# Masked attention and a rational feed-forward layer on one core: a third block in parts, another order of score products, another decoding of weights

## The chip, the core and the metric

The kernel runs on one core of a Trainium2 chip. The metric is the time of one execution on the device, in microseconds. The engines of the core have these names in the profile: PE is TensorE (products), PEld is TensorE's loading of weights, DVE is VectorE, ACT is ScalarE, POOL is GpSimd, SP is SyncE. Each engine works through its own list of instructions in order.

## The reference

Eight batches of eight heads, 576 positions, 64 values per head. A score below its row's maximum minus `tau` is dropped before the softmax. The output of the attention, 4608 rows of 512, goes through two layers with a rational function between them.

```python
scores = scale * np.matmul(q, k.transpose(0, 1, 3, 2))
thresh = np.max(scores, axis=-1, keepdims=True) - tau
scores = np.where(scores >= thresh, scores, -1000000000.0)
attn = np.exp(scores - np.max(scores, axis=-1, keepdims=True))
attn = attn / (np.sum(attn, axis=-1, keepdims=True) + 1e-09)
x = np.matmul(attn, v)                    # then to (4608, 512)
h = x @ w_in                              # (4608, 2048)
P = a[0] + a[1] * h + a[2] * h**2 + a[3] * h**3
Q = 1.0 + np.abs(b[0]) * np.abs(h) + np.abs(b[1]) * h**2
out = (P / (Q + 1e-6)) @ w_out            # (4608, 512)
```

The weights `w_in` and `w_out` come to the kernel as 64-bit floats, seen as pairs of 32-bit words.

## The kernel before

The kernel does not write its instructions down in order. It makes a list of small operations, each with an engine (or several that could take it, with a duration for each, in `FLEX`), a key that says how early it is wanted, the operations that it must follow, and the buffers that it takes and gives back. `Plan.order` then places them one by one on the engines by these assumed durations and latencies (`LAT`, `OWN`, `TO`), and the resulting order is the order of the instructions. Constants at the top (`WHEN`, `SPACING`, `EARLY`, `PRICE`, `TOL` and others) set the keys, the preference between engines, and how far a wanted operation may go before one that could start sooner.

**Attention.** A unit is 128 query positions of a pair of heads (four such units per pair, and half a unit for the remaining 64 positions). There are 128 full units. Its scores are made by `f_qk`: two products with 64 rows each, one for each head, on the two row halves of PE (L776; in float32 each shows as two records), and one product with all 128 rows for the remaining 64 keys of both heads (L780). Then DVE takes the maximum (L786), ACT applies threshold and exponential (L801, L805), the weights of the softmax are split in a high and a low f16 part (`f_hi`, L303 on ACT or L305 on DVE, and `f_lo`, L827), are transposed by DMA, and multiplied with V in column halves of PE (`f_av`, L896). For the first pairs the transposition is done by PE in float32 (`f_tr`, `f_avp`). V is split too (`vh`, `vl`, `vc`); the buffers of V need their empty corners set to zero again before each use (`f_zero`, L683, on DVE).

**Steps.** The two layers are done for 256 rows at a time (a chunk; 18 of them) and four blocks of 128 hidden units (a step, `moe_ops`). 72 steps result. Per step: 48 products in f16 for the first layer (L1013), ACT's reading of them (`f_h`, L1022), a chain of the rational function on tiles of 128 by 1024 in DVE and ACT (L1033 to L1055), and the second layer: two tiles of 128 rows times four blocks (`f_g2`). A block is done in one of two ways. Undivided: one float32 product with 512 columns (L1076), which shows as two records. In parts: the values and the weights are each split in a rounded part and a rest, and three products of the one-pass type `fp32r` are summed (L1072). Splitting the values takes a rounding (`f_gh`, a copy: L295 on ACT or L297 on DVE) and a difference (`f_gl`, L1063 on DVE), into one of two buffers `g`. Every second block is in parts:

```python
PARTS = 2
def in_parts(f):
    return f % PARTS == PARTS - 1
```

**Weights.** 16 pieces of `w_in` and 16 blocks of `w_out` are read by POOL's queue and decoded to float32 (`decode_ops`): `f1` scales the high word as a float (L303 or L305, out to `u`), `f2` reads the low word (L471), `f4` shifts by three bits (L475), `f5` puts the sign bit back (L479), `f6` adds the two (L310). A block in parts is then split (`f_wh`, `f_wl`, L567). `junk` takes the largest magnitude of a piece of `w_in` (L521). While PE would be idle in this time, dummy products on the identity are put in (`f_warm`, L1216).

**Buffers.** `t` (ten tiles of 128 by 1024) holds the loaded words and the three tiles of a step's chain; `u`, `e`, `hi`, `pT` and others serve the attention.

Of the kernel before, what the change touches and what calls it, by code (L numbers as in the profile page):

```python
# [17 lines left out]

REBIAS = 2.0 ** -112
QC = 1.0 + 1e-6  # L20

# [12 lines left out]
WHEN = [(-4.5639, 2.0326), (5.966, 0.8046), (12.6147, 0.2389), (15.3809, 0.834)]  # L34

V0, V1 = -1.2774, 1.1622

# [15 lines left out]

PARTS = 2

# [8 lines left out]

AHEAD_RANK = 2.4556

# [3 lines left out]

FLEX = {"f1": {"ACT": 0.567, "DVE": 0.335}, "f6": {"DVE": 0.6}, "s1": {"ACT": 0.648, "DVE": 0.396},
        "s2": {"DVE": 0.663}, "vmax": {"ACT": 0.697, "DVE": 0.729}, "thr": {"ACT": 0.242, "DVE": 0.122},
        "rec": {"ACT": 0.1, "DVE": 0.12}, "hi": {"ACT": 0.667, "DVE": 0.427}, "vh": {"ACT": 0.72, "DVE": 0.45},
        "vl": {"DVE": 0.795}, "xh": {"ACT": 0.264, "DVE": 0.335}, "xhr": {"ACT": 0.103, "DVE": 0.133},
        "ev": {"ACT": 0.465, "DVE": 0.6}, "ev1": {"ACT": 0.156, "DVE": 0.196}, "A": {"ACT": 0.583, "DVE": 0.341},
        "gh": {"ACT": 0.31, "DVE": 0.2}, "wh": {"ACT": 0.57, "DVE": 0.38}}
# [31 lines left out]
class Plan:  # L108

    LAT = {"PE": 0.27, "ACT": 0.28, "DVE": 0.22, "POOL": 0.16, "DMA": 2.3, "GD": 2.7}
    OWN = {"PE": 0.0, "ACT": 0.15, "DVE": 0.13, "POOL": 0.1, "DMA": 2.3, "GD": 2.7}
    TO = {("ACT", "DVE"): 0.23, ("ACT", "POOL"): 0.24, ("DVE", "ACT"): 0.2, ("DVE", "PE"): 0.3}

    def __init__(self):
# [3 lines left out]
        self.rank = 0.0  # L120

    def pool(self, name, n):
        self.pools[name] = [(0.0, i) for i in range(n)]

    def op(self, eng, dur, key, fn, after=(), take=(), drop=()):
        engs = {eng: dur} if isinstance(eng, str) else eng
        o = Op(engs, key, fn, [x for x in after if x is not None], list(take), list(drop))
        o.rank = self.rank
        self.ops.append(o)
        return o  # L130
# [20 lines left out]
    def order(self):  # L151
# [5 lines left out]
        engines = list(self.LAT)  # L157
        free = dict.fromkeys(engines, 0.0)
        can = {e: [] for e in engines}
        for o in self.ops:  # L160
# [11 lines left out]
        while left:  # L172
            best = None
            for e in engines:
                starts = []
                for o in can[e]:
                    t = max(free[e], o.ready[e])
                    for h in o.take:
                        spot = None if h.pool in line and line[h.pool][-1] is not h else self.spot(h, t)
                        if spot is None:  # L180
                            t = None
                            break
                        t = max(t, spot[0])
                    if t is not None:
                        starts.append((t, o))
                if not starts:
# [27 lines left out]
            free[e] = end = t + o.dur  # L214
            busy[e] += o.dur
            seen = end + self.LAT[e]
            for h in o.take:
# [36 lines left out]
def masked_attention_rational_ffn(  # L254
# [190 lines left out]
    def decode_ops(i, key, load, hold, dst=None):  # L445
# [27 lines left out]
        def f4():  # L473
            t = box["w"].bitcast(I32)
            nc.vector.tensor_single_scalar(t, t, 3, ALU.logical_shift_left)  # L475

        def f5():
            t = box["w"].bitcast(I32)
            nc.vector.scalar_tensor_tensor(t, box["rw"][:, :, 1], -0x80000000, t, ALU.bitwise_and, ALU.bitwise_or)  # L479

# [13 lines left out]
        o4 = op("DVE", 0.335, key, f4, [o1])  # L494
        o5 = op("DVE", 0.602, key, f5, [o4])
        o6 = op(FLEX["f6"], 0, key, f6, [o5, o2], (), [ht] if dst is None else [ht, hold])
        return o6, box
# [7 lines left out]
    for i in range(NW):  # L505
        pieces = []
        for c in range(NC):
# [12 lines left out]
            def junk(n=n, c=c, i=i, box=box):  # L520
                nc.scalar.activation(box["rw"][:, :, 0].bitcast(F32), box["w"], AF.Abs, accum_out=wm[:, i * NC + c:i * NC + c + 1])  # L521
            o7 = op("ACT", 0.66, key, junk, [o6], (), [hold])
            pieces.append((c, box, hold, o7))
# [20 lines left out]
    def in_parts(f):  # L544
        return f % PARTS == PARTS - 1

# [62 lines left out]
    def load_ops(bp, ts):  # L609
# [25 lines left out]
        q_done[bp] = [op(eng, 4.3 if first else 1.6, p0, ldq, (), [qh])]  # L635
        k_done[bp] = [op(eng, 0.1 if bp < FROM_ACT else 1.6, p0 + 0.1, ldk, (), [kh])]

# [6 lines left out]
    def v_low(bp):  # L644
        if bp not in v_done:
            p, o, vl, vc, vhi = v_ops[bp]
            o = op(FLEX["vl"], 0, p + 0.1, vl, [o] + plain_av.get(bp, []))
            v_done[bp] = op("DVE", 0.25, p + 0.15, vc, [o], (), [vhi])
        return v_done[bp]

    def load_v_ops(bp):
# [24 lines left out]
        q = bp * (NT + 0.5) - 17.0  # L676
        l = v_loaded[bp] = op(eng, 1.6, max(q, V0 + V1 * pr), ld, (), [vhold])
        hv = [Hold("u", 1)]

        def f_zero():  # L680

            for hh in range(2):
                nc.vector.memset(Vs[vhold.slot][hh * D:(hh + 1) * D, NT * P + (1 - hh) * D:NT * P + (2 - hh) * D], 0.0)  # L683
        if bp >= NV:
            l = v_loaded[bp] = op("DVE", 0.15, max(q, V0 + V1 * pr), f_zero, [l])
        vm_ops.setdefault(bb, []).append(op(FLEX["vmax"], 0, max(q + 1.0, p - 1.0 if bb else 3.0), mx, [l], hv, hv))
# [7 lines left out]
    def split_v_ops(bp):  # L694
# [9 lines left out]
        def high():  # L704
            return place(vhi).bitcast(F16)[:, 0:VW]
# [8 lines left out]
        def vc():  # L714
            nc.vector.tensor_copy(v_part(vh_[bp].slot, 1), high())  # L715
        o = op(FLEX["vh"], 0, p, vh, [isx_done[bb]], [vhi])
# [17 lines left out]
    def unit_ops(bp, t):  # L734
# [22 lines left out]
        def f_qk():  # L757
# [12 lines left out]
            box["s"][0], box["s"][1] = s[:, 0:S], s[:, w - S:]  # L770
            box["both"] = bass.AP(s.tensor, s.offset, [list(s.ap[0]), [w - S, 2], [1, S]])
            for hh in range(2):

                r = slice(hh * D, (hh + 1) * D)
                d = s[:, 0:NT * P] if hh == 0 else s[:, w - NT * P:]
                nc.tensor.matmul(d, QQ[r, t * P:(t + 1) * P], KK[r, REM:S], **one)  # L776
# [3 lines left out]
            nc.tensor.matmul(dst, QQ[:, t * P:(t + 1) * P], src, **one)  # L780

# [48 lines left out]
        def f_twice(part):  # L830

            x = box[part]
            nc.vector.tensor_copy(x[:, S:nb * P], x[:, NT * P:S])

# [97 lines left out]
        if plain:  # L932
# [5 lines left out]
            for piece in pieces:  # L938
                hold = Hold("b", 1, B1)
                tr = op("PE", 0.94 if piece < 2 else 0.35, p + 0.5, lambda x=piece, h=hold: f_tr(x, h), [dg], [hold],  # L940
                        [e_hold, dg_hold])
# [3 lines left out]
        else:  # L945
# [4 lines left out]
            if not full:  # L950
                his.append(op("DVE", 0.13, p + 0.55, lambda: f_twice("hi"), his))
                los.append(op("DVE", 0.13, p + 0.6, lambda: f_twice("lo"), los))
            tp = op("DMA", TPD if full else 0.6 * TPD, p + 0.6, lambda: f_tp("hi"), his + two["tp"], [two["pT"]] if t % 2 == 0 else (),
# [11 lines left out]
        if plain:  # L965
            av = op("PE", 2.36 if full else 0.76, p + 1.2, f_avp, two["tp"] + [v_loaded[bp], x_first.get(ck)], [bh] + first, [two["pT"], vh_[bp]])
            plain_av.setdefault(bp, []).append(av)
        else:
            av = op("PE", 1.86 if full else 0.69, p + 1.2, f_av, two["tp"] + [v_low(bp), x_first.get(ck)], [bh] + first, [two["pT"], vh_[bp]])
        x_first.setdefault(ck, av)  # L970
# [10 lines left out]
    def moe_ops(ck, f0, nb, p, begins, ends, soon):  # L981
# [122 lines left out]
        for j in range(nb):  # L1104
            for part in range(2):
                l1[j // 2] = prev = op("PE", 0.656, p + 0.1 * (2 * j + part), lambda j=j, part=part: f_g1(j, part),
                                       wi_done[g] + x_done[ck] + wo_done[f0:f0 + nb] + last_g1 if prev is None else [prev],
                                       [bhs[j // 2]] if (j % 2, part) == (0, 0) else (), [xo, xo])
# [150 lines left out]
```

## Time and profile before

| | |
|---|---|
| median of 3 runs | 1311.67 us (1310.85 to 1314.78) |
| profiled execution | 1315.6 us, its span 1313.8 us |
| PE busy | 1285.3 us, 9112 records |
| PEld busy | 866.0 us |
| DVE busy | 1200.6 us, 1981 instructions |
| ACT busy | 1064.5 us, 2094 instructions |
| POOL busy | 248.0 us, 474 instructions |
| mean granted clock of TensorE | 0.995 |

The span runs from the first to the last instruction. The ends of products are modelled in the profile, since products follow each other without a gap, so a busy PE need not be PE at its best pace. A group of instructions is given as line, engine, operation, what it writes and reads, shape, count, then its busy time and the mean of one in ns, then the idle time of the engine just before them with what ended it.

### The profile page before, as it was taken

Reading aid. Unit: us, or ns where it says so; the run is one execution under the profiler, and the core shown is the slowest. Engines: PE = TensorE matmul, PEld = TensorE weight load, DVE = VectorE, ACT = ScalarE, POOL = GpSimd, SP = SyncE. Lnnn points to the kernel's source line nnn. Section 1 sums busy time; section 2 is a strip of 40 time slices with the busy share of each in tenths; the row PEclk is TensorE's granted clock in tenths of the full one; section 3 lists DMA queues with packets and bytes.
Section 4 is the critical chain, followed back from the end, with each engine's and each line's share of the span. In section 5 each row is a group of like instructions: output and inputs, shape, how many; then the busy total and the mean of one; then the engine's idle time right before and its main releaser. Section 6 shows DMA issues by size and latency. Waiting matters only on the chain. (4 is left out here: it accounts for less than half of the span.)

```text
span 1313.8 us, 24744 instructions
## 1 busy us (share of the span) xinstructions
PE 1285.3 (98%) x9112; PEld 866.0 (66%) x9112; DVE 1200.6 (91%) x1981; ACT 1064.5 (81%) x2094; POOL 248.0 (19%) x474
## 2 busy tenths in 40 slices
PE   8988999999999999999999999999999999999998
PEld 6666676666666676666667576666667666677775
DVE  6989999999989999999988999999989999897766
ACT  5996989988988897778888798888887878874454
POOL 3211100023122321222111241322032211100000
PEclk9999999999999999999999999999999999999999
DMA  8532435676666664675663765775575746530000
GB/s 248 162 116 81 147 89 105 132 146 133 122 131 119 126 118 101 114 145 115 116 95 77 138 155 108 148 140 117 103 141 111 132 86 116 104 74 1 17 16 17
DMA packets 340585, 146.62 MB, mean 112 GB/s; under 512 B 316208, under 2 KB 323184, under 8 KB 340464
## 3 DMA queue, kind: packets, MB, share of 16 engines
q1 hardware_dynamic: 316400, 86.49, 37.8%
q0 software_dynamic: 22784, 57.31, 15.7%
q8 instruction: 72, 1.18, 0.4%
q10 hardware_dynamic: 1280, 1.25, 0.4%
q14 instruction: 49, 0.40, 0.1%
HBM read 60.30 MB, written 9.44 MB: 53 GB/s over the span
## 5 line engine op out<-in xcount | busy, mean ns | idle before, releaser
L1013 PEld LDWEIGHTS <-wi 128*128 128x128 f16 x3456 | 332.7, 98 | 64.8 <-issue 27.7
L1013 PE MATMUL banks<-x,wi 128*128 128x256 f16 x3072 | 360.2, 273 | 3.7 <-ACT pT L295 1.9
L1076 PE MATMUL banks<-wp,t 128*128 128x512 f32 x576 | 279.8, 601 | 2.3 <-DVE t L1055 2.1
L1072 PE MATMUL banks<-wp,g 128*128 128x512 f32 x864 | 276.4, 451 | 0.7 <-DVE g L1063 0.7
L805 ACT ACTIVATE e<-e,cf 128x576 f32<-128x576 f32 x288 | 221.1, 776 | 0.1
L801 ACT ACTIVATE e<-banks,st 128x576 f32<-128x576 f32 x288 | 206.2, 738 | 17.4 <-DVE st L795 12.0
L1072 PEld LDWEIGHTS banks<-wp,g 128*128 128x128 f32 x864 | 158.6, 189 | 78.5 <-issue 40.0
L827 DVE SCALAR_TENSOR_TENSOR e<-e,st,hi 128x576 f16<-128x576 f32 x252 | 204.2, 810 | 5.5 <-ACT hi L303 3.7
L303 ACT ACTIVATE hi<-e,st 128x576 f16<-128x576 f32 x192 | 144.7, 769 | 52.0 <-DVE st L816 42.3
L786 DVE TENSOR_REDUCE st<-banks 128x2 f32<-128x1152 f32 x128 | 172.3, 1346 | 10.3 <-PE banks L780 9.8
L776 PE MATMUL banks<-KK,QQ 64*128 64x512 f32 x512 | 151.3, 645 | 4.1 <-ACT e L801 3.5
L1076 PEld LDWEIGHTS banks<-wp,t 128*128 128x128 f32 x576 | 101.4, 190 | 74.2 <-issue 60.9
L1022 ACT ACTIVATE t<-banks,hsc 128x512 f32<-128x512 f32 (+1 forms) x192 | 106.4, 576 | 36.4 <-PE banks L1013 35.8
L896 PEld LDWEIGHTS <-V 128*64 128x64 f16 x2520 | 102.9, 111 | 28.9 <-issue 25.7
L896 PE MATMUL banks<-pT,V 128*64 128x256 f16 (+1 forms) x2520 | 121.0, 249 | 0.4 <-DVE V L715 0.4
L1049 DVE SCALAR_TENSOR_TENSOR t<-t,co,t 128x1024 f32<-128x1024 f32 (+1 forms) x73 | 92.2, 1263 | 30.5 <-ACT t L1043 30.5
L1040 ACT ACTIVATE t<-t,co 128x1024 f32<-128x1024 f32 (+1 forms) x73 | 82.6, 1132 | 36.3 <-DVE t L1046 36.2
L780 PEld LDWEIGHTS banks<-KK,QQ 128*128 128x128 f32 x256 | 38.3, 188 | 97.8 <-issue 87.9
L621 POOL DMA_DIRECT2D QQ<-in_qT_dram x42 | 22.4, 533 | 386.0 <-PE banks L767 227.8
L1033 DVE SCALAR_TENSOR_TENSOR t<-t,co 128x1024 f32<-128x1024 f32 (+1 forms) x73 | 92.1, 1262 | 2.2 <-ACT t L1022 2.2
L1055 DVE SCALAR_TENSOR_TENSOR t<-t,co,t 128x1024 f32<-128x1024 f32 (+1 forms) x73 | 92.2, 1264 | 0.8
L1046 DVE SCALAR_TENSOR_TENSOR t<-t,co,t 128x1024 f32<-128x1024 f32 (+1 forms) x73 | 92.1, 1262 | 0.0
(132 smaller groups left out, 1654.2 us busy)
## 6 DMA issues: line engine op xcount, KB each, us to landing
t<-in_w_in_dram POOLq DMA_DIRECT2D x16, 512.0 KB, 5.1
t<-in_w_out_dram POOLq DMA_DIRECT2D x16, 512.0 KB, 5.6
out_dram<-u POOLq DMA_DIRECT2D x26, 256.0 KB, 3.7
V<-in_v_dram POOLq DMA_DIRECT2D x24, 256.0 KB, 4.6
QQ<-in_qT_dram POOLq DMA_DIRECT2D x42, 144.0 KB, 2.8
KK<-in_kT_dram POOLq DMA_DIRECT2D x42, 144.0 KB, 4.0
QQ<-in_qT_dram POOLq DMA_DIRECT2D x42, 128.0 KB, 2.8
KK<-in_kT_dram POOLq DMA_DIRECT2D x42, 128.0 KB, 2.9
```

The costliest lines, as they stand in the source:

```text
L303: nc.scalar.activation(dst, src, AF.Identity, scale=factor)
L776: nc.tensor.matmul(d, QQ[r, t * P:(t + 1) * P], KK[r, REM:S], **one)
L786: nc.vector.tensor_reduce(box["st"][:, 0:2], box["both"], AX.X, ALU.max, negate=True)
L801: nc.scalar.activation(ev(hh), box["s"][hh], AF.Prelu, scale=SCALE, bias=box["st"][:, 2 + hh:3 + hh], alpha=STEEP)
L805: nc.scalar.activation(e, e, AF.Exp, scale=passes, accum_out=box["st"][:, 4 + hh:5 + hh])
L827: nc.vector.scalar_tensor_tensor(box["lo"][:, c], ev(hh), box["st"][:, 6 + hh:7 + hh], box["hi"][:, c], ALU.mult, ALU.subtract)
L896: nc.tensor.matmul(dst, V[:, c * P + hh * D:c * P + (hh + 1) * D], rhs, start=c == 0 and n == 0, stop=c == NT and n == 2)
L1013: nc.tensor.matmul(d, wi_tile(c, f0 + j, hl), x[:, c, :], start=c == 0 and n == 0, stop=c == NC - 1 and n == 2)
L1022: nc.scalar.activation(box["h3"][:, 2 * k:2 * k + 2, sl], psv[:, :, sl], AF.Identity, scale=hsc[:, b2, g:g + 1])
L1049: nc.vector.scalar_tensor_tensor(box["q"], box["q"], qc, box["i"], ALU.add, ALU.mult)
L1072: nc.tensor.matmul(acc[tt], fr(g[:, x]), fr(wo[f][y]), start=begins and j == n == 0, stop=ends and j == nb - 1 and n == 2)
L1076: nc.tensor.matmul(acc[tt], box["r"][:, o:o + P], wo[f], start=begins and j == 0, stop=ends and j == nb - 1)
```

## The change

Three things are done, and the planner's constants are set anew.

- Three of four blocks of the second layer are done in parts, not two. The four more divided weight blocks take 8 KB of each partition, and the pool `t` goes from ten tiles to eight.
- In `f_qk` of a full unit the product with all 128 rows is issued before the two with 64 rows.
- `f5` is gone. `f1` scales negative words by another 2^32, so that after the shift by three bits the sign bit stands where it belongs: one Prelu on ACT, or a product and a minimum on DVE.

Beside these: `f_zero` moves from DVE to POOL; `junk`, `vc` and `f_twice` may go to ACT or DVE; the planner knows a cost for changes of PE's tiling (`TURN`: f for all 128 rows and columns in float32, h the same in f16, r for row halves, c for column halves), and its durations of PE operations no longer contain those costs.

```diff
-POOLS = {"e": 3, "hi": 2, "pT": 2, "st": 8, "sc": 2, "t": 10, "u": 3, "g": 2, "x": 3, "xr": 1}
+POOLS = {"e": 3, "hi": 2, "pT": 2, "st": 8, "sc": 2, "t": 8, "u": 3, "g": 2, "x": 3, "xr": 1}
-LEAD, SPACE0, SPACING = 2.3618, 2.8866, 2.0262
-ENDK, ENDS = 6.3041, 10.3733
+LEAD, SPACE0, SPACING = 3.6093, 2.8146, 1.9783
+ENDK, ENDS = 5.6283, 6.2388
...
-PARTS = 2
+PARTS = 3
-AHEAD_RANK = 2.4556
+AHEAD_RANK = 1.5421
-EARLY = {"ACT": 1.7178, "DVE": 2.8692}
-EARLY_END = 1001.6266
-PRICE = {"ACT": 0.885, "DVE": 2.1934}
-TOL = {"PE": 0.08, "ACT": 0.1241, "DVE": 0.1, "POOL": 0.1, "DMA": 0, "GD": 0}
+EARLY = {"ACT": 2.4923, "DVE": 3.7394}
+EARLY_END = 1043.9074
+PRICE = {"ACT": 0.6141, "DVE": 2.3652}
+TOL = {"PE": 0.1187, "ACT": 0.1232, "DVE": 0.0398, "POOL": 0.1, "DMA": 0, "GD": 0}
+TURN = {("h", "r"): 0.095, ("f", "r"): 0.095, ("h", "c"): 0.095, ("f", "c"): 0.095, ("r", "h"): 0.1, ("r", "f"): 0.2,
+        ("c", "h"): 0.11, ("c", "f"): 0.2, ("r", "c"): 0.095, ("c", "r"): 0.095, ("h", "f"): 0.01}
...
-    LAT = {"PE": 0.27, "ACT": 0.28, "DVE": 0.22, "POOL": 0.16, "DMA": 2.3, "GD": 2.7}
+    LAT = {"PE": 0.27, "ACT": 0.28, "DVE": 0.22, "POOL": 0.16, "DMA": 2.8, "GD": 3.4}
...
+                        if e == "PE":
+                            t = max(t, free[e] + TURN.get((tiling, o.tiling[0]), 0.0))
...
-            times(box["w"], box["rw"][:, :, 1].bitcast(F32), REBIAS)
+            w, words_ = box["w"], box["rw"][:, :, 1].bitcast(F32)
+            if plan.eng == "ACT":
+                nc.scalar.activation(w, words_, AF.Prelu, scale=REBIAS, alpha=SIGN)
+            else:
+                nc.vector.tensor_scalar(w, words_, REBIAS, None, ALU.mult)
+                nc.vector.scalar_tensor_tensor(w, w, SIGN, w, ALU.mult, ALU.min)
...
-        def f5():
-            t = box["w"].bitcast(I32)
-            nc.vector.scalar_tensor_tensor(t, box["rw"][:, :, 1], -0x80000000, t, ALU.bitwise_and, ALU.bitwise_or)
...
     def in_parts(f):
-        return f % PARTS == PARTS - 1
+        return f % NC >= NC - PARTS
...
-                nc.vector.memset(Vs[vhold.slot][hh * D:(hh + 1) * D, NT * P + (1 - hh) * D:NT * P + (2 - hh) * D], 0.0)
+                nc.gpsimd.memset(Vs[vhold.slot][hh * D:(hh + 1) * D, NT * P + (1 - hh) * D:NT * P + (2 - hh) * D], 0.0)
...
+            dst, src = (bass.AP(x.tensor, x.offset, [list(x.ap[0]), [n, 2], [1, REM]])
+                        for x, n in ((s[:, NT * P:S], w - 2 * NT * P - REM), (KK[:, 0:REM], S)))
+            nc.tensor.matmul(dst, QQ[:, t * P:(t + 1) * P], src, **one)
             for hh in range(2):
-
                 r = slice(hh * D, (hh + 1) * D)
                 d = s[:, 0:NT * P] if hh == 0 else s[:, w - NT * P:]
                 nc.tensor.matmul(d, QQ[r, t * P:(t + 1) * P], KK[r, REM:S], **one)
-
-            dst, src = (bass.AP(x.tensor, x.offset, [list(x.ap[0]), [n, 2], [1, REM]])
-                        for x, n in ((s[:, NT * P:S], w - 2 * NT * P - REM), (KK[:, 0:REM], S)))
-            nc.tensor.matmul(dst, QQ[:, t * P:(t + 1) * P], src, **one)
...
-        qk = op("PE", 1.47 if full else 1.12, p, f_qk, need, [sh[0]], [kh, qh] * nh)
+        qk = plan.pe("fr" if full else "ff", 1.266 if full else 0.97, p, f_qk, need, [sh[0]], [kh, qh] * nh)
...
-            o = op("PE", 0.71 if j in hg else 0.865, p + 1.7 + 0.1 * i, lambda j=j, tt=tt: f_g2(j, tt),
+            o = op("PE", 0.705 if j in hg else 0.859, p + 1.7 + 0.1 * i, lambda j=j, tt=tt: f_g2(j, tt),
```

More of the change, by code (lines that the diff above doesn't have):

```diff
@@ L63 @@
 TPD = 1.3
-AHEAD_RANK = 2.4556
+AHEAD_RANK = 1.5421
 AHEAD = 3
 RECENT = 9.0
-FLEX = {"f1": {"ACT": 0.567, "DVE": 0.335}, "f6": {"DVE": 0.6}, "s1": {"ACT": 0.648, "DVE": 0.396},
+FLEX = {"f1": {"ACT": 0.567, "DVE": 0.94}, "junk": {"ACT": 0.66, "DVE": 0.62}, "f6": {"DVE": 0.6}, "s1": {"ACT": 0.648, "DVE": 0.396},
         "s2": {"DVE": 0.663}, "vmax": {"ACT": 0.697, "DVE": 0.729}, "thr": {"ACT": 0.242, "DVE": 0.122},
@@ L108 @@
 class Plan:
-    LAT = {"PE": 0.27, "ACT": 0.28, "DVE": 0.22, "POOL": 0.16, "DMA": 2.3, "GD": 2.7}
-    OWN = {"PE": 0.0, "ACT": 0.15, "DVE": 0.13, "POOL": 0.1, "DMA": 2.3, "GD": 2.7}
+    LAT = {"PE": 0.27, "ACT": 0.28, "DVE": 0.22, "POOL": 0.16, "DMA": 2.8, "GD": 3.4}
+    OWN = {"PE": 0.0, "ACT": 0.15, "DVE": 0.13, "POOL": 0.1, "DMA": 2.8, "GD": 3.4}
     TO = {("ACT", "DVE"): 0.23, ("ACT", "POOL"): 0.24, ("DVE", "ACT"): 0.2, ("DVE", "PE"): 0.3}
@@ L120, in __init__, with pe @@
         self.rank = 0.0
+    def pe(self, tiling, *args):
+        o = self.op("PE", *args)
+        o.tiling = tiling
+        return o
     def pool(self, name, n):
@@ L127, in op @@
         o = Op(engs, key, fn, [x for x in after if x is not None], list(take), list(drop))
-        o.rank = self.rank
+        o.rank, o.tiling = self.rank, "ff"
         self.ops.append(o)
@@ L158, in order @@
         free = dict.fromkeys(engines, 0.0)
+        tiling = "f"
         can = {e: [] for e in engines}
@@ L215, in order @@
             busy[e] += o.dur
+            if e == "PE":
+                tiling = o.tiling[1]
             seen = end + self.LAT[e]
@@ L714, in vc @@
         def vc():
-            nc.vector.tensor_copy(v_part(vh_[bp].slot, 1), high())
+            copy(v_part(vh_[bp].slot, 1), high())
         o = op(FLEX["vh"], 0, p, vh, [isx_done[bb]], [vhi])
@@ L832, in f_twice @@
             x = box[part]
-            nc.vector.tensor_copy(x[:, S:nb * P], x[:, NT * P:S])
+            copy(x[:, S:nb * P], x[:, NT * P:S])
         def f_tp(part):
```

37 lines of the change are left out of this document (20 added, 17 removed).

## The prediction

> **What bounds the kernel now.** I read the page's first two parts first, then busy time by stage, then the order of weight loads inside one step, then the groups.
>
> ```profile
> span 1313.8 us, 24744 instructions
> PE 1285.3 (98%) x9112; PEld 866.0 (66%) x9112; DVE 1200.6 (91%) x1981; ACT 1064.5 (81%) x2094; POOL 248.0 (19%) x474
> ...
> PE   8988999999999999999999999999999999999998
> ...
> DVE  6989999999989999999988999999989999897766
> ```
>
> The sum below is made against the profiled execution's own 1315.6 us (span 1313.8 and 1.8 around it); the median of the runs shown, 1311.67, lies 0.3% lower, and I take what I subtract off that median. 0.3% (4 us) is also about what a measurement of this kernel can tell from no change.
>
> ```profile
> core 0: us, PE busy (x) PEld busy (x) DVE busy (x) ACT busy (x) POOL busy (x), PEclk, DMA share, GB/s
> 200.00:1105.00 905.00, 899.97 (x6547) 595.53 (x6546) 863.04 (x1369) 777.25 (x1523) 206.66 (x381) 1.00 0.63 120
> 1105.00:1313.80 208.80, 203.14 (x1318) 140.95 (x1316) 160.63 (x206) 125.92 (x223) 10.54 (x20) 1.00 0.21 46
> 0.00:200.00 200.00, 182.20 (x1251) 129.53 (x1252) 176.91 (x407) 161.29 (x350) 30.75 (x73) 0.97 0.49 141
> ```
>
> There are three stages. **Start** (0 to 200): weights are decoded, PE lies idle for 17.8 us and fills more with dummy matmuls (166 of the 168 of L1216 are here, row below). **Middle** (to 1105): attention and the two-layer steps are interleaved; PE idles 5.0 us of 905, DVE 42, ACT 128. **Tail**: steps only; PE idles 5.7 of 208.8, DVE 48. So from 200 on a microsecond taken from PE is a microsecond of the span, as long as DVE and ACT can follow.
>
> ```profile
> L1216 PE MATMUL banks<-ident 128*128 128x128 f32 x166 | 25.7, 308 | 1.4 <-POOL ident masks.py:199 1.4
> L1076 PE MATMUL banks<-wp,t 128*128 128x512 f32 x24 | 12.4, 640 | 0.6 <-DVE t L1055 0.5
> L1076 PE MATMUL banks<-wp,t 128*128 128x512 f32 x420 | 204.4, 601 | 0.8 <-DVE t L1055 0.6
> L1076 PE MATMUL banks<-wp,t 128*128 128x512 f32 x132 | 63.0, 596 | 1.0 <-DVE t L1055 1.0
> ```
>
> One step has two undivided blocks of two products each, and each product shows as two records, so 8 records of L1076 are a step: 3 steps in the start, 52.5 in the middle, 16.5 in the tail, 72 in all.
>
> **The change, part by part.**
>
> *Third block in parts.* Per step one block goes from L1076 (one float32 product per token tile) to L1072 (three one-pass products).
>
> ```profile
> 606.45 0.19 PEld L1072 LDWEIGHTS banks<-wp,g 128*128 128x128 f32 x1 [0.24 <-DVE g L1063]
> 606.88 1.13 PEld L1072 LDWEIGHTS banks<-wp,g 128*128 128x128 f32 x5 [0.24 <-issue]
> 608.05 0.42 PEld L1076 LDWEIGHTS banks<-wp,t 128*128 128x128 f32 x2
> 608.71 0.19 PEld L1076 LDWEIGHTS banks<-wp,t 128*128 128x128 f32 x1 [0.24 <-issue]
> 609.14 0.19 PEld L1076 LDWEIGHTS banks<-wp,t 128*128 128x128 f32 x1 [0.24 <-issue]
> 609.57 0.19 PEld L1072 LDWEIGHTS banks<-wp,g 128*128 128x128 f32 x1 [0.24 <-issue]
> ```
>
> A weight load runs one matmul ahead, so the pace is read from load to load. The second L1076 load begins at 608.05 + 0.42 - 0.19 = 608.28. From there loads come every 0.43: an undivided block (four records) costs 4 x 0.43 = 1.72. The six records of a block in parts fill 606.88 to 608.28, 1.40. The gain is 0.32 per step: 0 in the start, where PE has slack, 52.5 x 0.32 = 16.8 in the middle, 16.5 x 0.32 = 5.3 in the tail.
>
> It adds work for the other two engines: per step one rounding (f_gh, line of copy: 295 on ACT, 297 on DVE) and one difference (L1063).
>
> ```profile
> L1063 DVE TENSOR_TENSOR g<-t,g 128x256 fp32r<-128x256 f32 x144 | 55.8, 417 | 1.2 <-ACT g L295 0.9
> L295 ACT CAST g<-t 128x256 fp32r<-128x256 f32 x84 | 31.9, 399 | 19.6 <-DVE t L1055 19.2
> L297 DVE CAST g<-t 128x256 fp32r<-128x256 f32 x60 | 16.3, 289 | 1.0
> L683 DVE MEMSET V<- 64x64 f32 x54 | 6.0, 112 | 1.4
> L305 DVE TENSOR_SCALAR hi<-e,st 128x576 f16<-128x576 f32 x60 | 30.7, 518 | 0.7
> L303 ACT ACTIVATE hi<-e,st 128x576 f16<-128x576 f32 x192 | 144.7, 769 | 52.0 <-DVE st L816 42.3
> ```
>
> In the middle that is 52.5 x 0.417 = 21.9 on DVE and, all on ACT, 52.5 x 0.399 = 20.9. The memsets that leave DVE for POOL give back some 4.5 (6.0 times the middle's three quarters). DVE and ACT held 863.0 + 777.3 = 1640 there; with 21.9 + 20.9 - 4.5 it is 1678. If PE alone set the pace the stage would last 905 - 16.8 - 4 (next paragraphs) = 884, and both would be busy 1678 of 1768, 94.9%.
>
> ```profile
> 200.00:300.00 100.00, 100.00 (x729) 65.70 (x729) 98.02 (x154) 90.77 (x178) 14.17 (x25) 1.00 0.64 131
> ```
>
> The densest of the nine hundreds from 200 to 1100 has 98.0 + 90.8 = 188.8 of 200, 94.4%. At that density 1678 takes 889. So I take 889, a gain of 16 in the middle; the ends are 884 and less (PE alone; a gain of 21 and more) and the DVE bound in the rivals. It asks DVE, which would need 880 of 889, to pass some 10 us to ACT: the rounding to f16 is 0.518 on DVE against 0.769 on ACT, and the copies of L715 and L833 can now move too.
>
> *Full-row product first.* In the kernel before, the two half-row products (L776) run first, then the 128-row one (L780).
>
> ```profile
> 611.48 0.30 PEld L776 LDWEIGHTS banks<-KK,QQ 64*128 64x128 f32 x4 [0.36 <-ACT e L805]
> 612.54 0.30 PEld L780 LDWEIGHTS banks<-KK,QQ 128*128 128x128 f32 x2 [0.76 <-issue]
> 612.75 0.54 PEld L1013 LDWEIGHTS <-wi 128*128 128x128 f16 x5
> ...
> L780 PEld LDWEIGHTS banks<-KK,QQ 128*128 128x128 f32 x256 | 38.3, 188 | 97.8 <-issue 87.9
> L1013 PEld LDWEIGHTS <-wi 128*128 128x128 f16 x3456 | 332.7, 98 | 64.8 <-issue 27.7
> ```
>
> L780's load comes 0.76 after the last half-row load ended: it does not run ahead, it waits for the half-row products to end, and its own 0.188 lies bare. After L780 the first-layer load follows at 0.21, not held. Turned round, L780's load can run ahead under what precedes it, and the bare load is that of the next operation: 0.098 for a first-layer f16 product, 0.19 for a float32 one. So a unit gains at most 0.188 - 0.098 = 0.09, and nothing when float32 follows. 256/2 = 128 units, 101 in the middle: between 0 and 9; I take 4 there (half), none elsewhere. A unit that follows a product in column halves (L896) may pay one held load more, 0.19; were that so for one in four, the 4 would be gone. The page "TensorEngine Tiling (Array Packing)" of the Trainium skill (Key Properties) says that a change of tiling mode drains TensorE; the trace agrees (the 0.76 at L780). By that rule alone, with two changes a unit before and after, the reorder is worth nothing, and the best case below would be 1279 in place of 1270.
>
> *Decoding without the sign.* 32 pieces lose one DVE operation (L479); the scaling becomes a Prelu on ACT, or on DVE two operations.
>
> ```profile
> L479 DVE SCALAR_TENSOR_TENSOR u<-t,u 128x512 int32<-128x512 int32 x32 | 21.7, 685 | 0.2
> L305 DVE TENSOR_SCALAR u<-t 128x512 f32<-128x512 f32 x22 | 9.1, 421 | 0.2
> L303 ACT ACTIVATE u<-t 128x512 f32<-128x512 f32 x10 | 6.8, 681 | 4.2 <-DMA t<-in_w_in_dram 2.2 <-PE banks L408 2.0
> L567 DVE TENSOR_TENSOR wp<-t,wp 128x512 fp32r<-128x512 f32 x8 | 5.4, 684 | 0.5 <-ACT wp L295 0.5
> ```
>
> On DVE the new form is 0.421 + 0.685 = 1.11, as dear as before, so I put the 22 on ACT at 0.68: DVE -21.7 - 9.1, ACT +15. Four more divided weight blocks add 4 x 0.684 on DVE and as much on ACT, three steps 0.8 each. Start's DVE and ACT held 338; now 338 - 21.7 - 9.1 + 15 + 5.4 + 2.4 = 330, 4 us less for each of the two. I take 4. The ends: 15 (DVE alone bound, and PE has the slack for it) and a loss of 10, from the buffers:
>
> ```profile
> POOL t L513 <- DVE wi L537: 20.7, 2, 15.2
> ```
>
> *Buffers t, 10 to 8.* These loads of weights already wait for a t buffer's last reader; with two fewer they start later. A step takes three of the eight, and its first writer L1022 waits for PE (35.8 of its 36.4 us idle, row below), not for a buffer, so I cost it at nothing in the middle, hidden by PE; without that cover it is the loss named.
>
> ```profile
> L1022 ACT ACTIVATE t<-banks,hsc 128x512 f32<-128x512 f32 (+1 forms) x192 | 106.4, 576 | 36.4 <-PE banks L1013 35.8
> POOL V L659 <- PE banks L896: 181.8, 18, 19.6
> PEld banks L1072 <- DVE g L1063: 3.9, 12, 1.3
> ```
>
> *Memsets to POOL.* 54 short ones behind the V loads. That queue waits 181.8 us for PE to free a V slot, so the Q, K and V loads that stand behind the memset, and the score products that read them, are early anyway: nothing, and without that cover a load's few us in the start, 5 at worst. *Order numbers* (keys, prices, tolerances, the new tiling costs): no row shows them. PE idles 5.0 + 5.7 outside the start, so a better order can give 10.7 at most; as much may be lost; I take 0.
>
> Sum: middle 16 + tail 5.3 + start 4 = 25.3; 1315.6 - 25.3 = 1290.3 for an execution like the profiled one, 1311.7 - 25.3 = **1286 us** for the median.
>
> **Rivals.**
>
> *DVE is the bound already.* PE's ends are modelled, so its 98% may be padding; its loads are busy 66%, and DVE at 91% would lead. Then only DVE's sum counts: -21.7 - 9.1 - 6.0 + 72 x 0.417 + 2.7 = -4, so 1308, no change. Against it: in the middle DVE idles 42 and PE 5, and the loads of L1076 stand at exactly 0.43 apart with "issue" before them, not DVE. The page "Perfetto Trace Analysis" of the Trainium skill (Identifying the Most-Contended Engine) holds matmul busy time to be a poor measure and prefers the share of weight loads, which is what speaks for this rival; the spacing of the loads in this trace does not agree with it.
>
> *DVE becomes the bound.* If the order leaves on DVE what it holds, it needs 880 in the middle. At its densest, 98.0%, this is 898: a gain of 7, 5.3 and 4 elsewhere, 1295. For it: DVE's load grows where it is fullest. Against: ACT has 128 us free.
>
> *Slower: the two g slots.* A step now has three divided blocks and still two g slots, so the third block's rounding waits until the first block's products are done, then 0.399 + 0.417 and three hand-overs, against 1.40 of the second block's products. With a 1.27 us DVE operation of the chain in front (92.1 us for 73, row below) it comes 0.399 + 0.417 + 1.27 - 1.40 = 0.69 late, with the hand-overs some 0.8 (an estimate); 69 steps x 0.8 = 55 less the 25 gives 1341. It decides from 25.3 / 69 = 0.37 us a step on. For it: the third slot is not added. Against: PE waits for L1063 only 3.9 us now, and first-layer and score products can be put between.
>
> ```profile
> L1033 DVE SCALAR_TENSOR_TENSOR t<-t,co 128x1024 f32<-128x1024 f32 (+1 forms) x73 | 92.1, 1262 | 2.2 <-ACT t L1022 2.2
> ```
>
> *Better than forecast.* PE alone sets the pace (884 and all of the reorder, 879) and the start gains 10: 26 + 5.3 + 10 = 41, 1270.
>
> **How the numbers follow.** Forecast 0.58 (1278 to 1294, by 8 us of start and order); better 0.12; DVE becomes the bound 0.14; DVE bound already 0.07; g slots 0.09. The range reaches from 1268 (better) to 1304 (DVE bound with half of the start's loss); it leaves out most of the last two and a little on the other side. Faster by over 0.3% holds the first three, 0.84; within it 0.07; slower 0.09.
>
> **What would show it.** L1072 at 1296 records and L1076 at 288, their paces unchanged; L479 gone; L1063 at 216; in the middle ACT's share up by 5 points or more and DVE at 97%; the bare load after L776 now that of L1013. Wrong if PE's idle time in the middle grows past 20 us, with waits of L1072 for L1063 (g slots) or of first-layer products for L912 and L1055 (DVE), or if the start grows.

## The result, and the profile after

The changed kernel takes 1303.08 us (median of 4, 1299.74 to 1303.94) against 1313.06 (median of 4) for the kernel before: 0.992 of it, interval 0.9895 to 0.9946. That is 10 us less, 7 to 14 by the interval, where 25 were forecast. The way was right, the size was not. Below, a kernel's gain or loss against the changed kernel is the difference of their ratios to the kernel before, times 1313; a ratio's interval is some 0.2 to 0.3% to each side, 3 to 4 us, so that such a gain or loss below some 5 us is not clear of the noise. The expectations use differences of medians in two places: 7.5 and 3 there are 5.8 and 2.8 here, 16.5 is 17.3.

The page of the changed kernel's profiled execution (1302.46 us), the lines that answer to those of before:

```profile
span 1300.5 us, 25214 instructions
PE 1255.9 (97%) x9272; PEld 896.6 (69%) x9272; DVE 1196.5 (92%) x1930; ACT 1089.7 (84%) x2210; POOL 255.7 (20%) x525
...
PE   5989899999999999999999999999999999999998
...
DVE  2887899999999999999999899999999999897776
...
L1087 PE MATMUL banks<-wp,g 128*128 128x512 f32 x1296 | 359.6, 419 | 2.1 <-DVE g L1078 2.1
...
L1091 PE MATMUL banks<-wp,t 128*128 128x512 f32 x288 | 141.1, 606 | 3.9 <-DVE t L1070 3.8
...
L309 ACT CAST g<-t 128x256 fp32r<-128x256 f32 x143 | 55.0, 402 | 46.6 <-DVE t L1070 25.3
...
L1078 DVE TENSOR_TENSOR g<-t,g 128x256 fp32r<-128x256 f32 x216 | 87.2, 426 | 3.2 <-ACT g L309 2.6
```

Span is busy time and idle time of PE. Before: 1285.3 + 28.5. Now: 1255.9 + 44.6. PE's busy time fell by 29.4, where 26.1 were forecast (16.8 + 4 + 5.3), and 16.1 of it came back as idle time. Busy time by stage, the kernel before first, says where:

```profile
0.00:50.00 50.00, 44.85 (x266) 32.66 (x268) 35.48 (x97) 35.30 (x79) 16.65 (x48) 0.93 0.87 253
200.00:1100.00 900.00, 894.97 (x6502) 592.00 (x6501) 858.30 (x1363) 773.41 (x1515) 206.66 (x381) 1.00 0.63 120
```

```profile
0.00:50.00 50.00, 33.38 (x199) 25.23 (x199) 22.70 (x58) 26.52 (x56) 10.16 (x35) 0.83 0.60 165
200.00:1100.00 900.00, 888.70 (x6690) 626.54 (x6689) 880.91 (x1355) 792.17 (x1610) 215.75 (x427) 1.00 0.63 120
```

The columns are PE, PEld, DVE, ACT, POOL, the granted clock, the DMA engines' share and GB/s. In the first 50 us PE's idle time went from 5.2 to 16.6, and DVE and ACT were busy 13 and 9 us less as well. By 200 us 2.5 of these 11.4 are made up (PE idles 26.7 us of the first 200, 17.8 before). In the middle it went from 5.0 to 11.3, while DVE rose to 880.9 of 900, 97.9%. The last operation of each step's chain (L1055 before, L1070 now) gives the two ends of the steps:

```profile
L1055 DVE SCALAR_TENSOR_TENSOR t<-t,co,t x73: 751/1278/1286, 109.3 to 1304.2; 128x1024 f32<-128x1024 f32 x71, 128x512 f32<-128x512 f32 x2
```

```profile
L1070 DVE SCALAR_TENSOR_TENSOR t<-t,co,t x73: 752/1285/1324, 119.9 to 1291.0; 128x1024 f32<-128x1024 f32 x71, 128x512 f32<-128x512 f32 x2
```

The first step is 10.6 late, the last 13.2 early: 23.8 were won between them, and 10.6 were lost before them. These are two single executions; their spans differ by 13.3, the medians by 10.0, so the 23.8 may be some 3 too much.

The start of the changed kernel in order of time (start, duration, engine, line; a small q marks an engine's queue issuing a transfer):

```profile
3.60 0.59 SPq L676 DMA_DIRECT2D V<-in_v_dram  x1
...
5.46 0.59 SPq L676 DMA_DIRECT2D V<-in_v_dram  x1
...
7.30 0.59 SPq L676 DMA_DIRECT2D V<-in_v_dram  x1
...
7.96 1.13 PE L795 MATMUL banks<-KK,QQ 64*128 64x512 f32 x4
...
9.75 0.60 SPq L638 DMA_DIRECT2D QQ<-in_qT_dram  x1
...
16.21 0.47 ACTq L645 DMA_DIRECT2D KK<-in_kT_dram  x1
...
19.02 0.47 ACTq L647 DMA_DIRECT2D KK<-in_kT_dram  x1
...
19.54 0.78 ACT L820 ACTIVATE e<-e,cf 128x576 f32<-128x576 f32 x1 [6.53 <-DMA V<-in_v_dram]
...
20.45 0.17 DVE L827 TENSOR_SCALAR st<-st 128x2 f32<-128x2 f32 x1 [8.14 <-ACT e L820]
...
26.82 0.77 PE L791 MATMUL banks<-KK,QQ 128*128 128x128 f32 x2 [12.93 <-DMA KK<-in_kT_dram]
27.51 2.08 PE L795 MATMUL banks<-KK,QQ 64*128 64x512 f32 x4
```

Three V loads go out ahead of the second pair's Q load, and its K loads, which ACT's queue issues, go out only from 16.21 to 19.02, while the profile shows ACT waiting for a V load. ACT stands 6.5 us there, DVE 8.1 behind ACT, and PE 12.9 for K. The cause is in the order numbers, in a line of the full diff that the excerpt ahead of the prediction does not show:

```diff
-V0, V1 = -1.2774, 1.1622
+V0, V1 = -1.9936, -0.6323
```

With V1 below zero the keys of the V loads of pairs 1 to 3 (`max(q, V0 + V1 * pr)`, -2.6 to -3.5) lie below that of the second pair's Q load, -2.0. In the kernel before, the second pair's Q loads come first (4.93) and the V loads after them; the scores of the second pair start at 12.20:

```profile
4.93 0.62 SPq L621 DMA_DIRECT2D QQ<-in_qT_dram  x1
...
6.87 0.59 SPq L659 DMA_DIRECT2D V<-in_v_dram  x1
...
12.20 1.75 PE L776 MATMUL banks<-KK,QQ 64*128 64x512 f32 x4
```

### The profile page after: what moved, and what is told of

Same layout as the page of the kernel before. It is cut to its first block, busy times and chain, and to the rows that moved or that the text cites. A ratio compares the mean times of both kernels' runs of the same rounds, so it can differ in the third digit from the quotient of the medians.

```text
span 1300.5 us, 25214 instructions
## 1 busy us (share of the span) xinstructions
PE 1255.9 (97%) x9272; PEld 896.6 (69%) x9272; DVE 1196.5 (92%) x1930; ACT 1089.7 (84%) x2210; POOL 255.7 (20%) x525
## 4 chain that ended last, share of the span: by engine, by line
PE 44%; DVE 13%; issue 4%; ACT 3%; DMA 1%; POOL 0%; DVEq 0%; SPq 0%; ACTq 0%; POOLq 0%
PE banks L1028 14%; PE banks L1087 13%; PE banks L1091 5%; PE banks L911 4%; PE banks L795 4%; DVE e L842 2%; PE banks L784 2%; DVE st L801 1%; DVE t L1064 1%; PE banks L791 1%; DVE t L1051 1%; DVE t L1070 1%; DVE t L1048 1%; DVE t L1061 1%; DVE t L1067 1%
## 5 line engine op out<-in xcount | busy, mean ns | idle before, releaser
L1028 PEld LDWEIGHTS <-wi 128*128 128x128 f16 x3456 | 327.7, 98 | 108.9 <-issue 73.0
L1028 PE MATMUL banks<-x,wi 128*128 128x256 f16 x3072 | 365.5, 273 | 5.8 <-ACT t L1037 4.5
L1087 PE MATMUL banks<-wp,g 128*128 128x512 f32 x1296 | 359.6, 419 | 2.1 <-DVE g L1078 2.1
L1087 PEld LDWEIGHTS banks<-wp,g 128*128 128x128 f32 x1296 | 235.1, 188 | 105.3 <-issue 38.5
L801 DVE TENSOR_REDUCE st<-banks 128x2 f32<-128x1152 f32 x128 | 173.3, 1354 | 14.0 <-PE banks L795 13.2
L317 ACT ACTIVATE hi<-e,st 128x576 f16<-128x576 f32 x183 | 139.7, 772 | 45.4 <-DVE st L831 38.6
L795 PE MATMUL banks<-KK,QQ 64*128 64x512 f32 x512 | 146.6, 650 | 0.0
L1091 PE MATMUL banks<-wp,t 128*128 128x512 f32 x288 | 141.1, 606 | 3.9 <-DVE t L1070 3.8
L1064 DVE SCALAR_TENSOR_TENSOR t<-t,co,t 128x1024 f32<-128x1024 f32 (+1 forms) x73 | 92.6, 1272 | 23.8 <-ACT t L1058 23.7
L1055 ACT ACTIVATE t<-t,co 128x1024 f32<-128x1024 f32 (+1 forms) x73 | 82.9, 1136 | 14.3 <-DVE t L1061 13.6
L309 ACT CAST g<-t 128x256 fp32r<-128x256 f32 x143 | 55.0, 402 | 46.6 <-DVE t L1070 25.3
L1048 DVE SCALAR_TENSOR_TENSOR t<-t,co 128x1024 f32<-128x1024 f32 (+1 forms) x73 | 92.8, 1271 | 0.9 <-ACT t L1037 0.5
L1070 DVE SCALAR_TENSOR_TENSOR t<-t,co,t 128x1024 f32<-128x1024 f32 (+1 forms) x73 | 92.8, 1272 | 0.6
L1061 DVE SCALAR_TENSOR_TENSOR t<-t,co,t 128x1024 f32<-128x1024 f32 (+1 forms) x73 | 92.9, 1273 | 0.0
L1051 DVE SCALAR_TENSOR_TENSOR t<-t,co 128x1024 f32<-128x1024 f32 (+1 forms) x73 | 92.8, 1271 | 0.0
L1078 DVE TENSOR_TENSOR g<-t,g 128x256 fp32r<-128x256 f32 x216 | 87.2, 426 | 3.2 <-ACT g L309 2.6
```

The lines of the kernel that those rows point to most:

```text
L317: nc.scalar.activation(dst, src, AF.Identity, scale=factor)
L801: nc.vector.tensor_reduce(box["st"][:, 0:2], box["both"], AX.X, ALU.max, negate=True)
L1028: nc.tensor.matmul(d, wi_tile(c, f0 + j, hl), x[:, c, :], start=c == 0 and n == 0, stop=c == NC - 1 and n == 2)
L1061: nc.vector.scalar_tensor_tensor(box["r"], box["r"], a1, box["h"], ALU.add, ALU.mult)
L1087: nc.tensor.matmul(acc[tt], fr(g[:, x]), fr(wo[f][y]), start=begins and j == n == 0, stop=ends and j == nb - 1 and n == 2)
L1091: nc.tensor.matmul(acc[tt], box["r"][:, o:o + P], wo[f], start=begins and j == 0, stop=ends and j == nb - 1)
```

## The experiments

Two theories. "Start": the missing microseconds went into that first wait. "Density": in the middle PE and DVE are both so full that neither's relief shows.

**The second pair's loads first.** The changed kernel's plan is kept, but two of its operations, the first Q and K loads of the second pair, are issued right behind the first pair's.

```diff
+        if (bp, ts) == visits[1]:
+            second = k_done[1] + q_done[1]
...
-    for o in plan.order():
+    placed = plan.order()
+    second = [o for o in placed if o in second]
+    rest_ = [o for o in placed if o not in second]
+    for o in rest_[:2] + second + rest_[2:]:
```

A kernel that took `k_done[1] + q_done[1]` as they stand after all visits moved the loads of the pair's second visit instead, and those of the first stayed behind the V loads. It does not test the theory, and its 1303.28 us are the changed kernel's. Expected of it:

> The changed kernel with one thing moved: the Q and K loads of the second pair are issued ahead of the four V loads instead of behind and between them; every engine's order of computing is unchanged. Theory 'start': the 11.5 us by which PE's idle time in the first 50 us grew (16.6 against 5.2) comes from those loads landing at 26 us; PE idle in 0 to 50 goes back to 5 to 8 us and the kernel gains 8 to 12 us, to some 1292. Rival 'density' (the gain was lost in the middle, where DVE is 98% busy): the time stays within 3 us of 1303, what the start wins is waited for later.

The kernel of the lines above:

> The changed kernel with the first Q and K loads of the second pair issued ahead of the four V loads; all computing is in the same order. Theory 'start': PE idle in 0 to 50 goes from 16.6 back to 5 to 8 us, the first steps come 10 us earlier and the end with them: 1290 to 1295. Rival 'density': the start gains as much, but the middle, where DVE is 98% and PE 99% busy, gives it back: over 1298.

1293.87 us, ratio 0.9855 (0.9835 to 0.9875): 8.5 us gained. Its first 50 us, and its steps:

```profile
0.00:50.00 50.00, 42.30 (x269) 31.64 (x269) 31.60 (x83) 36.32 (x80) 13.12 (x41) 0.93 0.77 221
...
L1070 DVE SCALAR_TENSOR_TENSOR t<-t,co,t x73: 752/1279/1296, 110.1 to 1283.3; 128x1024 f32<-128x1024 f32 x71, 128x512 f32<-128x512 f32 x2
```

PE idles 7.7 in place of 16.6, and nearly all of the 8.9 appears at the end. The first step comes at 110.1, 9.8 earlier than in the changed kernel and 0.8 later than in the kernel before. "Start" holds for this part.

**K from SP's queue.** `kq_ = nc.scalar if bp < 1 else queue`, V loads still ahead.

> The changed kernel, with the second pair's K loads issued from SP's queue in place of ACT's; V loads stay ahead. If the harm is that ACT stands behind a K load that cannot be issued yet (6.5 us idle before its next exponential), this gains 4 to 7 us. If the harm is only that the Q and K loads land late, the scores of the second pair still wait until about 26 us and the gain is under 2 us.

1297.02 us, 0.9885 (0.9861 to 0.9909): 4.6 gained, about the size of the noise. ACT's wait of 6.5 us is gone from its trace (the exponential runs at 13.04), and the second pair's scores start 2.5 us earlier too (PE's wait ends at 24.35, not 26.82). Taken as it stands, about half of the loss came from issuing in ACT's list; how much of that is ACT standing still and how much the earlier scores, this run does not part.

**The mirror.** The kernel before, with the V loads of pairs 1 to 3 issued ahead of the second pair's.

> The mirror: the kernel before with the V loads of pairs 1 to 3 issued ahead of the second pair's Q and K loads, all computing in the same order. Theory 'start': PE idle in 0 to 50 rises from 5.2 by 6 to 12 us and the kernel loses 5 to 12 us. Rival: before has work to spare in the start (PE ran 25.7 us of dummy products), so it loses under 2 us.

1317.26 us, 1.0034 (1.0022 to 1.0046): 4.5 lost, a little under the range. The dummy products are no reserve; a late start is late to the end.

**Less of one engine, less of two.** Four kernels leave work of the changed kernel out: the DVE operation of L1067; the third product of block 1; both; the exponential of L1058 on ACT.

```diff
-            nc.vector.scalar_tensor_tensor(box["q"], box["q"], -2.0, box["i"], ALU.add, ALU.mult)
+            return
...
-                for n, (x, y) in enumerate(((0, 0), (1, 0), (0, 1))):
+                for n, (x, y) in enumerate(((0, 0), (1, 0), (0, 1))[:2 if f % NC == 1 else 3]):
```

> The changed kernel without the 73 DVE operations of L1067 (a factor of the reciprocal's correction is left out), 89 us of DVE's work; PE's work is unchanged. If PE sets the pace, at most PE's idle time of the middle (11.3 us) and a little of the start can be gained: 0 to 12 us. If DVE sets the pace (rival 'density'), 30 us or more are gained.

> The changed kernel without the third product of the newly divided block (the rounded value times the weight's rest is left out for block 1 of each step): 144 PE products of 0.233, 33.6 us of PE's work, DVE and ACT unchanged. If PE sets the pace the kernel gains 24 to 33 us. If DVE sets it, under 8 us.

> The changed kernel with both reliefs at once: without the operations of L1067 (89 us of DVE) and without the third product of block 1 (33.6 us of PE). Each alone gained 7.5 and 3 us. If PE and DVE hold each other, so that either keeps the pace when the other is relieved, the two together gain clearly more than 10.5: 20 to 33 us, to 1270 to 1283. If neither is the pace (ACT or hand-overs are), about 10 us.

> The changed kernel without the second ACT pass of the reciprocal (the exponential of L1058 is left out), 75 us of ACT's work and one link of each step's chain from DVE to ACT and back; PE and DVE unchanged. If ACT or the chain through it sets the middle, 15 us or more are gained; if PE and DVE do, under 8.

Less DVE: 1295.53 us, 0.9876 (0.9847 to 0.9905), 5.8 gained. Less PE: 1300.1, 0.9899 (0.9867 to 0.993), 2.8 gained. Less ACT: 1299.73, 0.9903 (0.9888 to 0.9918), 2.2 gained. Both: 1269.03, 0.9675 (0.9658 to 0.9692), 32.2 gained, nearly four times the sum of the two. Of the single ones only the 5.8 is clear of the noise, and barely; that all lie below 8 speaks against any one of the three engines as what sets the pace. The middle with less PE, then with less of both:

```profile
200.00:1100.00 900.00, 874.72 (x6569) 603.69 (x6569) 876.62 (x1350) 785.64 (x1600) 214.53 (x427) 1.00 0.64 120
```

```profile
200.00:1100.00 900.00, 888.97 (x6766) 622.26 (x6764) 845.87 (x1338) 811.02 (x1656) 223.21 (x445) 1.00 0.65 125
```

With less PE, its idle time grows to 25 and DVE stays where it was; only with DVE relieved too does PE fill up again, and more gets done in the same 900 us. PE and DVE hold each other: the 33.6 us of PE's work are worth 2.8 with DVE as it is, and 26.4 (32.2 - 5.8) with DVE relieved.

**Was it so before?** The same third product of block 1 left out of the kernel before.

> The kernel before without the third product (rounded value times the weight's rest) of block 1 of each step: 144 PE products of 0.233, 33.6 us of PE's work, nothing else changed. The prediction's premise (from 200 us on, a microsecond taken from PE is a microsecond of the span): 28 to 33 us gained. If PE and DVE hold each other already in the kernel before, where DVE is 95% busy in the middle: 3 to 12 us.

1303.71 us, 0.9932 (0.9914 to 0.995): 8.9 of 33.6 us, 27%. So PE alone did not set the pace before either. That DVE, at 95%, was what held it is likely from the runs on the changed kernel, but not shown: no run takes DVE's work out of the kernel before.

**The score products alone.** In the kernel before only the order of the three products is turned; in the changed kernel it is turned back.

> The kernel before with one edit: in each full unit the 128-row product ahead of the two half-row products; all orders around it unchanged. By the prediction's rows: 54 units are followed by first-layer products (0.09 each), 18 by column-half products (one switch less, some 0.2 each), and 17 come after column halves (one switch more, 0.2): 5 us of PE. If PE sets the pace, 1313 less 3 to 7. The rule that a switch drains, two before and two after, gives 0; 'density' (DVE holds) gives 0 to 2.

> The changed kernel with only the order of a full unit's score products turned back (half-row products first). In the kernel before the turn did nothing (ratio 1.0015). Here 42 units are followed by the first rows of a block in parts and 44 by first-layer products; if PE's tiling switches are what the new plan uses, 3 to 8 us are lost; if not, within 2 us of 1303.

Before turned: 1314.52 us, 1.0015 (0.9996 to 1.0033). Changed turned back: 1301.62, 0.9916 (0.9899 to 0.9934), the changed kernel's 0.992. Nothing either way. In the turned kernel before the middle reads:

```profile
200.00:1100.00 900.00, 890.25 (x6499) 597.70 (x6497) 858.23 (x1363) 772.91 (x1515) 207.13 (x381) 1.00 0.62 120
```

PE's busy time falls by 4.7, about the 5 that were expected. The ends in that sum are modelled, but the weight loads at a unit with the same neighbours in both kernels agree: from the start of the loads of L1072 ahead of the unit to the first load of the value product behind it they take 4.92 us before (610.00 to 614.92) and 4.84 turned (610.10 to 614.94), 0.08 less, close to the 0.09 forecast for a unit. At the next three units it is 0.00, 0.10 and 0.09. None of it reaches the span.

**The sign operation.** Issued again in the changed kernel, and left out of the kernel before (whose weights lose their signs).

```diff
             nc.vector.tensor_single_scalar(t, t, 3, ALU.logical_shift_left)
+            nc.vector.scalar_tensor_tensor(t, box["rw"][:, :, 1], -0x80000000, t, ALU.bitwise_and, ALU.bitwise_or)
```

> The changed kernel with the sign operation issued again after each shift (its result changes nothing): 32 DVE operations of 0.685, 22 us of DVE's work in the first 200 us, the order otherwise unchanged. If the start is set by DVE, 10 to 20 us are lost. If by loads and hand-overs, as DVE's 153 us of 200 says, 0 to 5.

> The kernel before with its sign operation left out (the weights lose their signs), 32 DVE operations of 0.685 less in the first 200 us, all orders unchanged. The prediction priced this relief at 4 us of the start. The experiment that issued the operation again in the changed kernel lost 16.5; if the start is a chain through DVE in both kernels, this gains 10 to 18 us.

Issued again: 1319.63 us, 1.0052 (1.0035 to 1.007), 17.3 lost for 22 us of DVE. Left out before: 1312.95, 0.9997 (0.998 to 1.0014), nothing gained, against the expectation of 10 to 18. Its one profiled execution does have the first step 4.3 earlier (105.0 against 109.3), but that execution is among the shorter of its ten, and with other variants of the kernel before the first step lies anywhere from 107.6 to 112.2. An order that was made for given durations may pay for what is added and not collect what is taken away; that is a reading of these two runs, not shown by them. Neither number is the price of this part of the change.

**The third block.** Once planned anew with two blocks (`PARTS = 2` in the changed kernel), once at the changed kernel's order, with block 1's three products replaced by one float32 product of the rounded parts (the rests of block 1 are left out).

```diff
+                if f % NC == 1:
+                    nc.tensor.matmul(acc[tt], g[:, 0], wo[f][0], start=False, stop=False)
+                    return
```

> The changed kernel planned anew with two blocks of four in parts (blocks 2 and 3) in place of three; t stays at eight tiles and all else is the changed kernel's. This prices the third block. PE theory of the prediction: 23 us of PE come back, of which 16 to 23 show: 1319 to 1326. 'Density' (PE, DVE and ACT all near full, no one of them the pace): PE gets 23 us more, DVE some 31 and ACT 29 less; within 6 us of 1303.

> The changed kernel with the three one-pass products of block 1 replaced by one float32 product of the two rounded parts (the rests of block 1 are left out of the sum); DVE, ACT and all orders unchanged. It prices the PE side of the third block without planning anew: 72 steps x 0.32 = 23 us of PE's work come back. PE theory: 16 to 23 us lost. If PE and DVE hold each other, relief of PE is worth little, but work added to a full engine costs nearly all of itself: 12 to 23 us lost as well; under 6 only if PE is not near the pace at all.

Planned anew: 1348.97 us, 1.0285 (1.0264 to 1.0306), 48 more, outside both ranges. The page:

```profile
PE 1285.1 (95%) x9152; PEld 882.1 (66%) x9152; DVE 1182.0 (88%) x1846; ACT 1063.4 (79%) x2145; POOL 254.0 (19%) x525
```

PE is busy 29.2 us more than in the changed kernel (24 of its records more are dummy products), but the span is 45.2 longer: 16 us are idle time. The likely reason, not tested, is an order whose constants fit another kernel. So this prices the plan as much as the block. At the fixed order: 1320.4, 1.0056 (1.0037 to 1.0075), 17.9 lost. Its page:

```profile
PE 1275.9 (97%) x9128; PEld 870.2 (66%) x9128; DVE 1200.7 (91%) x1930; ACT 1091.9 (83%) x2210; POOL 255.0 (19%) x525
```

That is 20.0 more of PE's work, of which nine tenths show. Both theories expected about this, so it does not decide between them.

**A version faster than both.** The second pair's loads first, and the V loads in the order of the pairs.

> A version to beat both: the changed kernel with the second pair's Q and K loads ahead of the V loads and the four V loads issued in the order of the pairs (0 to 3, not 3 to 0), since pair 0's product needs the first of them. Theory 'start': as good as with the one change alone (1293.9) or 1 to 3 us better, 1290 to 1294. Rival: the largest value over all four V is waited for anyway, so no difference.

1292.12 us, 0.9846 (0.9823 to 0.987): 9.7 under the changed kernel, 1.5% under the kernel before. From the kernel with the first change alone it can't be told apart.

## Why the prediction missed the size

*"Order numbers ... I take 0"* is the step that failed first. It bounded them by 10.7 in either direction from PE's idle time outside the start, and did not look at the one number that moves transfers in the start. V1 with its sign stood in the full diff, and its keys could be worked out. It cost 8.5 to 9.7 us. That this is less than 10.7 is luck, since the bound was made for the stages outside the start.

*The start's term* (4 gained, ends 15 and -10) is the second. Measured at the first step, it was to come 4 earlier and came 10.6 later, 14.6 off. With the second pair's loads in front it comes 0.8 later than before, so 9.8 of the 14.6 are those loads; the other 4.8 are the 4 that the start was to gain and 0.8 more; no run says why they did not come. The reason given for a loss in the start, the t buffers, was not the one found, and they were not tried alone. Between first and last step 23.8 were won (some 21 if the medians' difference holds), where 16 + 5.3 were forecast. So measured, the whole shortfall lies in the start.

*"From 200 on a microsecond taken from PE is a microsecond of the span"* was wrong for the kernel before: 27% of it. The sentence carried its condition ("as long as DVE and ACT can follow"), and the term for the middle was then set by density, not by PE; but the reader was left with PE as the bound, and the tail's 5.3 and the better end (884) rest on it. PE's 5 us of idle and DVE's 42 were taken for bound and reserve. About half of DVE's 42 was waiting for ACT inside the softmax (9.7 us behind L805, 9.6 behind L810); that this time could not be used in that order is a reading, not shown. The step had the mechanism wrong, but it cost the sum little, since the middle went by density.

*The density term* (94.4%, 889 us) named the engines that mattered, though DVE and ACT reached 92.9% from 200 to 1100 (880.9 + 792.2 of 1800). PE's paces were right: float32 at 0.43 a record (605.22, 605.65, 606.08 below), one-pass at 0.233 (eleven loads in 2.52). That the sum from first to last step fits is not proof of its parts: at fixed orders the PE side of the third block is worth 17.9 as a burden, and by the kernel before some 27% of 23, about 6 (an estimate), as a relief.

```profile
605.22 0.19 PEld L1091 LDWEIGHTS banks<-wp,t 128*128 128x128 f32 x1 [0.24 <-issue]
605.65 0.19 PEld L1087 LDWEIGHTS banks<-wp,g 128*128 128x128 f32 x1 [0.24 <-ACT hi L317]
606.08 2.52 PEld L1087 LDWEIGHTS banks<-wp,g 128*128 128x128 f32 x11 [0.24 <-DVE g L1078]
608.64 0.42 PEld L791 LDWEIGHTS banks<-KK,QQ 128*128 128x128 f32 x2
609.18 0.30 PEld L795 LDWEIGHTS banks<-KK,QQ 64*128 64x128 f32 x4
610.24 1.23 PEld L1087 LDWEIGHTS banks<-wp,g 128*128 128x128 f32 x6 [0.76 <-ACT e L820]
```

*The reorder's 4 us* became nothing in the span. The held load moved from L791 to the operation after the unit, with the same 0.76, as the rows show. By the rule of the page "TensorEngine Tiling (Array Packing)" of the Trainium skill (Key Properties), a drain at each change of mode, the reorder is worth nothing either. The span agrees but can't tell that rule from density, and the loads show 0.00 to 0.10 saved at four units: PE's side was about as forecast, and what failed is that PE's time is the span's.

*The decoding's 4 us* can't be confirmed: nothing in the medians when taken from the kernel before, 17.3 lost when given back to the changed one.

Of the rivals, "DVE becomes the bound" (1295, chance 0.14) came nearest in time, and DVE did reach 97.9% in the middle. But it put the loss there, with 12.3 left for middle and tail, where some 21 to 24 were won. So 1303 lying at the slow end of the range (1304, from this rival and a loss in the start) is in part luck. Of the signs that were named for being wrong, "if the start grows" came true. ACT took most of the roundings (143 of 216, L309), but its busy share in the middle rose by 2 points (773.4 to 792.2 of 900), not 5. The g slots cost PE little: its weight loads waited 7.3 us for L1078 in all.

```profile
PEld banks L1087 <- DVE g L1078: 7.3, 20, 2.2
ACT g L309 <- PE banks L1087: 20.6, 17, 2.1
```

ACT now stands 20.6 us for a free slot, at 84% busy. What stays open: how the 10 us divide between the third block, the decoding and the new order, since prices taken at a fixed order depend on whether work is added or removed; and what two t tiles fewer cost.

## What to carry to other kernels

When two engines are both over 95% busy, relieve one alone in the kernel as it is before counting on the gain: here 33.6 us of PE's work were worth 8.9 before and 2.8 after (the latter within the noise), and with 89 us of DVE's taken away as well the two were worth 32, though DVE's alone had given 5.8. In a kernel ordered by a planner, read a change of its constants as a list of moved instructions, transfers first: one sign in a key cost as much as the whole change won. ACT, which also issues transfers, stood 6.5 us here at loads that did not go out; at the start, give each load the place in which it is first needed.

## What the runs showed of the hardware

Loads to be issued held ACT for 6.5 us ahead of an exponential that, with the issue moved to SP, ran at 13.04 in place of 19.54; that move gave 4.6 us back, the earlier scores included. After PE had stood for 12.9 us, the same four score records took 2.08 us in place of 1.13 (27.51 and 7.96 above), and the granted clock of the first 50 us fell from 0.93 to 0.83. The page "TensorE: Matmul & The Clock Gate" of the Trainium skill (Part 1: The HAM clock gate) says that the clock drops to half after an idle window; the trace comes near, with a factor of 1.84 between the two durations.
